# Fewer copied score pairs, and VectorE's side work placed between the score copies, in a fused attention and SwiGLU kernel

## Chip, cores and metric

One core of a Trainium2 chip runs the whole kernel. The metric is the time of one execution on the device in microseconds (us). PE is TensorE's matrix multiplier, PEld its weight load, DVE is VectorE, ACT is ScalarE, POOL is GpSimd, SP is the engine whose queue issues most DMAs.

## What is computed

```
xn = layernorm(x)                                  # x: 2048 tokens x 512
q, k, v = split(xn @ wqkv)                         # 32 heads of 16
o  = softmax(q @ k.T * 16**-0.5) @ v               # every head, 2048 x 2048 scores
s  = o @ wo
h  = silu(xn @ w_gate) * (xn @ w_up)               # 1792 wide
g  = silu(h @ w_down)
out = x + s * g
```

Inputs and outputs are float32. The kernel splits operands of a product into a rounded high part and the remaining low part and sums three products (high x high, high x low, low x high). Making such a pair costs DVE one copy (the rounding) and one subtraction.

## The kernel before

A first part (some 160 us) normalises x and projects q, k and v. Then comes the main loop, which is one instruction order written out by hand: each engine executes its instructions in the order in which the program emits them.

**Units and blocks.** Attention is cut into 32 units: 8 groups of 4 heads, times 4 slices of 512 queries. A unit goes over 16 tiles of 128 keys (kt). It is cut into 3 or 4 blocks of 4 to 6 key tiles, 100 blocks in all (`run`). A key tile has two pairs of heads, so a block of n tiles has 2n pairs, and each pair needs two score matmuls (128 x 512 each).

**Fill.** A block also carries f steps of other work, one step being two matmuls on the two row halves of the array (`both`, into `bankx` and `banky`): 24 steps for the gate and up projection of one 128-wide slice of the hidden layer, 21 for one token tile of the down projection, 9 or 12 for the output projection near the end. `events(n, f)` writes the order of a block as marks in slots: F is a fill step, D a direct pair, A and B the two halves of a copied pair. A slot is the time of one F or one D, half a slot that of an A or a B.

- A **direct** pair (D) goes into one of two double banks `score`, and ACT takes the exponential straight from there (L846).
- A **copied** pair (A, then B) goes one score at a time through the single bank `acc[1]` (`spare_bank`). DVE copies A out (L858); only then can B be written; DVE copies B out (L863). ACT takes the exponential of the copied pairs in place, at the end of the block (L865).

The tiles of exponentials, `pr`, come from a pool of 11 buffers; each is free again when `values` (L370) has multiplied it with v. `values` runs for the whole block after its events, tile by tile, with the copied pairs last. So PE's order is: events of a block, values of the block, events of the next.

The number of copied pairs follows from n and f; length = 2n + f:

| blocks | n | f | copied, of 2n |
|---|---|---|---|
| 31 | 5 | 24 | 1 |
| 23 | 5 | 21 | 2 |
| 22 | 6 | 24 | 3 |
| 7 | 6 | 21 | 4 |
| 11 | 4 | 12 | 3 |
| 2 | 4 | 9 | 4 |
| 2 and 2 | 4 | 21, 24 | 1, 0 |

That makes 214 copied pairs out of 1024.

**DVE's other work.** In a block with 24 fill steps the last step is followed by ACT's tanh (L212) and DVE's two gating steps (L213, L214), which free `bankx` and `banky`; then DVE splits the hidden slice `hh` (L169, L170, `split_hidden`) and the rows of w_down, `wd` (L147, L148, `split_wd`). `split_gu` (L136, L138) splits the gate and up weights of the next slice; its four pieces are emitted at every fourth fill step. At a unit's end `finish` turns `acc[0]`, divides by the softmax sum (`normalise`, L377, L380, L384), and for every second group turns the result back (L391) and, for the last group, splits it (`split_o`, L270, L271); all of that is emitted in one go after the second D of the next unit's first block. SP loads the weights two slices ahead (`load_gu`) and one slice of w_down (`load_wd`), whose single buffer `wdr` is free when `split_wd` has read it.

Of the kernel before, what the change touches and what calls it, by code (L numbers as in the profile page):

```python
# [9 lines left out]
F32 = mybir.dt.float32  # L10
# [9 lines left out]
P = 128  # L20
# [3 lines left out]
DH = 16  # L24
F = 1792
NB = 4
TB = S // NB
# [23 lines left out]
def tile_block(ctx: ExitStack, tc: tile.TileContext, x, wqkv, wo, w_gate, w_up, w_down, out):  # L51
# [71 lines left out]
    def load_gu(i):  # L123
# [3 lines left out]
            sp.dma_start(raw[j * HALF:(j + 1) * HALF], w[:, f * P:(f + 1) * P].rearrange("(c p) f -> p c f", p=HALF))  # L127
        gu[i] = [raw]

    def split_gu(i):  # L130
        raw = gu[i][0]
        hi = two.tile([P, DC, P], F32R, tag="guh", name="guh")
        lo = two.tile([P, DC, P], F32R, tag="gul", name="gul")
        gu[i] = (hi, lo)
        for h in (slice(0, DC // 2), slice(DC // 2, DC)):
            dve.tensor_copy(hi[:, h], raw[:, h])  # L136
            yield
            dve.tensor_sub(lo[:, h], raw[:, h], hi[:, h].bitcast(F32))  # L138
            yield

    def load_wd(i):
        raw = one.tile([P, D], F32, tag="wdr", name="wdr")
# [1 line left out]
        wdr[i] = raw  # L144

    def split_wd(f, i):
        dve.tensor_copy(wd[:, f, 0], wdr[i])  # L147
        dve.tensor_sub(wd[:, f, 1], wdr[i], wd[:, f, 0].bitcast(F32))  # L148

    def load_fx(b, j):  # L150
        for h in range(2):
# [13 lines left out]

    def split_hidden():
        while kept:
            f, i, ga = kept.pop(0)
            dve.tensor_copy(hh[:, f, 0], ga)  # L169
            dve.tensor_sub(hh[:, f, 1], ga, hh[:, f, 0].bitcast(F32))  # L170
            split_wd(f, i)

    halves = [slice(h * HALF, (h + 1) * HALF) for h in range(2)]

# [16 lines left out]
    def ffn(b):  # L191
        for grp, part in enumerate(GROUPS):
            nf = part.stop - part.start
            for f in range(nf):
                i = b * NF + part.start + f
                pieces = split_gu(i + 1) if i + 1 < NB * NF else iter(())
                if i + 2 < NB * NF:
                    load_gu(i + 2)
                hi, lo = gu.pop(i)
                n = 0  # L200
                for c in range(DC):
                    for wt, j in ((hi, 0), (hi, 1), (lo, 0)):
                        both(wt[:, c], fx[:, j, c], n == 0, n == 3 * DC - 1)
                        n += 1
                        if n % 4 == 2:
                            next(pieces, None)
                        if n == DC and i:
                            load_wd(i)
                        if n == 3 * DC:
                            th = one.tile([P, TB], F32, tag="th", name="th")  # L210
                            ga = two.tile([P, TB], F32, tag="ga", name="ga")
                            act(th, bankx, AF.Tanh, scale=0.5)  # L212
                            dve.scalar_tensor_tensor(ga, th, 1.0, bankx, op0=ALU.add, op1=ALU.mult)  # L213
                            dve.scalar_tensor_tensor(ga, ga, 0.5, banky, op0=ALU.mult, op1=ALU.mult)  # L214
                            kept.append((f, i, ga))
                            if now >= 0:
                                split_hidden()
                            if grp == 1 and f == nf - 1 and b + 1 < NB:
                                load_fx(b + 1, 0)
                                load_fx(b + 1, 1)  # L220
                            elif grp == 1 and f == nf - 1:
                                load_wo(0)
                        yield 3 * DC - n
            for t in range(NT):
                n = 0
                for f in range(nf):
                    for a, w in ((0, 0), (0, 1), (1, 0)):
                        both(hh[:, f, a, t * P:(t + 1) * P], wd[:, f, w], n == 0, n == 3 * nf - 1)
                        n += 1
                        if n == 3 * nf and grp == 0:  # L230
                            dve.tensor_copy(facc[:, t], bankx)
                            dve.tensor_add(facc[:, t], banky, facc[:, t])
                        elif n == 3 * nf:
                            y = two.tile([P, D], F32, tag="ga", name="y")
                            dve.tensor_add(y, bankx, facc[:, t])
                            dve.tensor_add(y, banky, y)
                            after.append(partial(store_gate, y, b * TB + t * P))
                            if b == NB - 1:
                                after.append(partial(next_out, t))
                        yield 3 * nf - n  # L240
# [132 lines left out]
    def normalise(u, first, last, between=None):  # L373
        g, b = divmod(u, NB)
        n = last - first
        o1 = late.tile([P, TB], F32, tag="o1", name="o1")
        dve.transpose(o1[:, :n], acc[0][:, first:last])  # L377
        ov = o1[:, :n].rearrange("p (c d) -> p c d", d=32)
        rl = late.tile([P, TB // 32], F32, tag="rl", name="rl")[:, :n // 32]
        dve.reciprocal(rl, ov[:, :, DH])  # L380
        if between:
            between()
        dst = on[b][:, first:last].rearrange("p (c s d) -> p c s d", s=2, d=DH)[:, :, g % 2]
        dve.tensor_mul(dst, ov[:, :, :DH], rl[:, :, None].to_broadcast([P, n // 32, DH]))  # L384

    def finish(u):
        g, b = divmod(u, NB)
        normalise(u, 0, TB)
        if g % 2:
            o2 = late.tile([P, TB], F32, tag="o2", name="o2")  # L390
            dve.transpose(o2, on[b])  # L391
            if g < NG - 1 or b == NB - 1:
                pool.dma_start(o_d[g // 2, b], o2)
            else:
                whole = (hh, wd, hh)[b].rearrange("p f j t -> p (f j) t")
                lhs[b, DT - 1] = whole[:, 2 * (DT - 1)], whole[:, 2 * DT - 1]
                split_o(lhs[b, DT - 1], o2)
                ready[b] += 1

    settled = mybir.DependencyInfo(mybir.DependencyClass.Sync, mybir.DependencyReason.DATA)  # L400
    units = NG * NB
# [45 lines left out]

    def events(n, f):
        length = 2 * n + f
        copied = max(0, 2 * n - max(2, (4 * length - 6) // 16 + 1)) if f else 0  # L450
        direct = 2 * n - copied
        gap = max(4, min(5, (length - 8) / max(1, direct - 2)))
        marks = [(0, "D"), (1, "D")] + [(7 + gap * i, "D") for i in range(direct - 2)]
        marks += [(4 + (length - 6) * i / (2 * copied), "AB"[i % 2]) for i in range(2 * copied)]
        marks.sort()
        out = []
        at = left = 0
        for t, kind in marks:
            while left < f - 1 and at < t:
                out.append("F")  # L460
                left += 1
                at += 1
            out.append(kind)
            at += 1 if kind == "D" else 0.5
        return direct, out + ["F"] * (f - left)


    with ExitStack() as pro:
        pc = pro.enter_context(tc.tile_pool(name="pc", bufs=1))
# [210 lines left out]
        for b in range(NB):  # L680
# [3 lines left out]
            for n, (make, i) in enumerate(slots):  # L684
# [9 lines left out]
                if b == 2 and n == 8:  # L694
                    load_wd(0)
                if not more and n == 2:
                    for _ in split_gu(0):
                        pass
                    for bank in acc:
                        dve.memset(bank, 0.0)  # L700
                if not more and n in (1, 3):
# [40 lines left out]
                if not more and n == 9:  # L742
# [6 lines left out]
                    for h in range(2):  # L749
                        dve.tensor_copy(selq[:, h * HALF:h * HALF + 1], s4)  # L750
                    fill(3 * DC)
                    low, high = [pps.tile([P, 512], F32, tag="ps", name="low") for _ in range(2)]
                    mm(high[:2 * NG * NB, :8], sel, row[:, :8], start=True, stop=True, skip_group_check=True)
                    mm(low[:HALF + 2, :8], selq, row[:, :8], start=True, stop=True, skip_group_check=True)
# [59 lines left out]

    now = 0
    split_hidden()
    ends = []

    def run(u, first, n):
# [4 lines left out]
        direct, todo = events(n, f)  # L824
        if now == 0:
            for _ in range(4):
                todo.insert(0, todo.pop(len(todo) - 1 - todo[::-1].index("F")))
        pairs = [(kt, j) for kt in range(first, first + n) for j in range(2)]
        straight, copies = pairs[:direct], pairs[direct:]
        probs, waiting = {}, []  # L830
# [4 lines left out]
            mm(bank, k[r, j, kc * P:(kc + 1) * P], q[r, j], start=True, stop=True)  # L835

        done = 0
        for e in todo:
            if e == "F":
                fill(1)  # L840
            elif e == "D":
# [10 lines left out]
            elif e == "A":  # L852
                kt, j = copies.pop(0)
                waiting.append((kt, j))
                scores(spare_bank, kt, j, 0)
                lower = True
                probs[kt, j] = ppool.tile([P, 2, TB], F32, tag="pr", name="pr")
                dve.tensor_copy(probs[kt, j][:, 0], spare_bank)  # L858
            else:
                kt, j = waiting[-1]  # L860
                scores(spare_bank, kt, j, 1)
                lower = False
                dve.tensor_copy(probs[kt, j][:, 1], spare_bank)  # L863
        for kt, j in waiting:
            act(probs[kt, j], probs[kt, j], AF.Exp, scale=0.25)  # L865
        out_splits()
        catch_up()
        values(u, range(first, first + n), probs)
# [51 lines left out]
    for t, c in ((2, 0), (2, 1), (2, 2), (3, 0)):  # L920
        products(t, c)
    for n in range(2):
        normalise(units - 1, n * half, (n + 1) * half, partial(low, 0) if n else None)
        turned.append(spare[:, n])
        dve.transpose(turned[n][:, :half], on[NB - 1][:, cols[n]])
        nc.scalar.copy(hi[:, cols[n]], turned[n][:, :half])
# [38 lines left out]
```

## Time and profile before

| | |
|---|---|
| median of 3 runs | 1583.88 us (1583.39 to 1585.63) |
| the profiled execution | 1583.19 us |
| its span, first to last instruction | 1581.4 us |
| busy: PE, PEld, DVE, ACT | 1520.2, 890.6, 829.0, 1098.2 us |
| direct exponentials | 810, 1027 ns each |
| exponentials of copied pairs | 214, 1060 ns each |
| score copies | 2 x 214, 690 and 692 ns each |

In the views, a row of the timeline gives start, duration, engine, line, operation, out<-in, shape and count of a run of like instructions, and in brackets the idle time of the engine before it with what ended that. Rows of PE overlap, since matmuls are pipelined. In a windows row the figures after the length are each engine's busy time, then the granted TensorE clock (1.00 is full), DMA share and GB/s.

### The profile page before, as it was taken

The numbers are of one execution on the slowest core, as the hardware profiler recorded it, in microseconds if no ns is written. First come the engines' busy times: TensorE is split into PE (matmuls) and PEld (weight loads), VectorE is DVE, ScalarE is ACT, GpSimd is POOL, SyncE is SP. The second block draws the span as 40 slices with busy tenths as digits, with TensorE's granted clock in tenths as the row PEclk, the third lists the DMA queues.
The fourth block names the chain that finished last, engine by engine and source line by source line (L and its number), as shares of the span: only waits on it lengthen the run. The fifth ranks groups of instructions, "written<-read, shape, count | busy, mean of one in ns | idle before, by whom it ended". The sixth has DMA issues, their size and how long they took to land.

```text
span 1581.4 us, 27925 instructions
## 1 busy us (share of the span) xinstructions
PE 1520.2 (96%) x11227; PEld 890.6 (56%) x11227; DVE 829.0 (52%) x1439; ACT 1098.2 (69%) x1235; POOL 89.4 (6%) x104
## 2 busy tenths in 40 slices
PE   9999799999999999999999999999999999888887
PEld 7787555555556555555565455565655555333333
DVE  5543454456546645554566355546554545554545
ACT  6633477777877777777877677787767776645543
POOL 4100100000000000000000000000000000001222
PEclk9999899999999999999999999999999999877978
DMA  6678521143624311444243034722321223122131
GB/s 220 235 251 245 129 67 32 38 114 76 138 64 117 80 32 31 102 100 112 68 108 75 11 72 100 154 74 71 92 65 37 66 58 91 51 84 80 61 100 48
DMA packets 126957, 148.18 MB, mean 94 GB/s; under 512 B 12524, under 2 KB 79340, under 8 KB 126052
## 3 DMA queue, kind: packets, MB, share of 16 engines
q1 hardware_dynamic: 121620, 125.79, 31.7%
q0 software_dynamic: 4912, 20.12, 3.4%
q8 instruction: 91, 1.49, 0.4%
q14 instruction: 46, 0.38, 0.1%
q10 hardware_dynamic: 288, 0.39, 0.1%
HBM read 106.68 MB, written 39.58 MB: 92 GB/s over the span
## 4 chain that ended last, share of the span: by engine, by line
PE 85%; DVE 8%; ACT 4%; issue 2%; DMA 1%; SPq 0%; DVEq 0%; ACTq 0%
PE acc L370 29%; PE bankx L182 18%; PE score L835 12%; PE banky L182 9%; PE acc L835 7%; PE ps L591 5%; ACT pr L846 3%; DVE pr L858 3%; PE ps L593 3%; DVE pr L863 1%; DVE o L377 1%; ACT pr L865 0%; DVE o L391 0%; PE acc L566 0%; DMA v_d<-vt 0%
## 5 line engine op out<-in xcount | busy, mean ns | idle before, releaser
L846 ACT ACTIVATE pr<-score 128x1024 f32<-128x1024 f32 x810 | 778.7, 1027 | 384.6 <-PE score L835 322.4
L370 PE MATMUL acc<-pr,vst 128*17 128x512 f32 x4096 | 510.0, 606 | 0.0
L835 PE MATMUL score<-qst,kst 50*128 50x512 f32 x1620 | 411.3, 419 | 0.0
L182 PE MATMUL banky<-fx,guh 64*128 64x512 f32 x896 | 319.8, 399 | 0.0
L182 PE MATMUL bankx<-fx,guh 64*128 64x512 f32 x896 | 312.3, 395 | 0.1
L370 PEld LDWEIGHTS acc<-pr,vst 128*17 128x17 f32 x4096 | 114.2, 98 | 343.5 <-issue 273.5
L858 DVE COPY pr<-acc 128x512 f32<-128x512 f32 x214 | 147.6, 690 | 206.0 <-PE acc L835 193.6
L835 PEld LDWEIGHTS score<-qst,kst 50*128 50x128 f32 x1620 | 187.3, 187 | 118.4 <-issue 74.0
L835 PE MATMUL acc<-qst,kst 50*128 50x512 f32 x428 | 200.0, 467 | 52.0 <-DVE pr L858 32.8
L863 DVE COPY pr<-acc 128x512 f32<-128x512 f32 x214 | 148.0, 692 | 139.2 <-PE acc L835 135.4
L865 ACT ACTIVATE pr<-pr 128x1024 f32<-128x1024 f32 x214 | 214.5, 1060 | 0.0
L182 PE MATMUL bankx<-wd,hh 64*128 64x512 f32 x672 | 205.8, 395 | 0.0
L182 PE MATMUL banky<-wd,hh 64*128 64x512 f32 x672 | 196.5, 394 | 0.0
L182 PEld LDWEIGHTS bankx<-fx,guh 64*128 64x128 f32 x896 | 167.6, 187 | 16.7 <-issue 0.9
L182 PE MATMUL bankx<-fx,gul 64*128 64x512 f32 x448 | 176.9, 395 | 0.0
L182 PE MATMUL banky<-fx,gul 64*128 64x512 f32 x448 | 176.6, 394 | 0.0
L182 PEld LDWEIGHTS banky<-fx,guh 64*128 64x128 f32 x896 | 165.7, 187 | 2.7
L835 PEld LDWEIGHTS acc<-qst,kst 50*128 50x128 f32 x428 | 81.4, 190 | 131.3 <-DVE pr L858 64.8
L213 DVE SCALAR_TENSOR_TENSOR ga<-th,bankx 128x512 f32<-128x512 f32 x56 | 38.5, 688 | 195.7 <-ACT th L212 195.7
L182 PEld LDWEIGHTS bankx<-wd,hh 64*128 64x128 f32 x672 | 124.1, 186 | 12.6
L182 PEld LDWEIGHTS banky<-wd,hh 64*128 64x128 f32 x672 | 124.3, 186 | 6.1
L182 PEld LDWEIGHTS bankx<-fx,gul 64*128 64x128 f32 x448 | 84.4, 188 | 6.9
(165 smaller groups left out, 1381.3 us busy)
## 6 DMA issues: line engine op xcount, KB each, us to landing
gur<-in_B_w_gate_dram SPq DMA_DIRECT2D x56, 256.0 KB
gur<-in_B_w_up_dram SPq DMA_DIRECT2D x56, 256.0 KB
wdr<-in_B_w_down_dram SPq DMA_DIRECT2D x56, 256.0 KB
kst<-k_d SPq DMA_DIRECT2D x192, 64.0 KB
qst<-q_d SPq DMA_DIRECT2D x192, 64.0 KB
fx<-xt_d SPq DMA_DIRECT2D x24, 512.0 KB
q_d<-parts SPq DMA_DIRECT2D x16, 512.0 KB
k_d<-parts SPq DMA_DIRECT2D x16, 512.0 KB
```

The source lines that it names most:

```text
L182: mm(banks[i], lhs[halves[i]], rhs[halves[i]], start=start, stop=stop)
L213: dve.scalar_tensor_tensor(ga, th, 1.0, bankx, op0=ALU.add, op1=ALU.mult)
L370: mm(acc[0][h * 32:h * 32 + DH + 1], v[:, kt % CT, h * (DH + 1):(h + 1) * (DH + 1)], probs[kt, h // 2][:, h % 2], start=kt == 0, stop=kt = ...
L377: dve.transpose(o1[:, :n], acc[0][:, first:last])
L591: mm(ps, w, a[:, c], start=n == 0, stop=n == 3 * DT - 1)
L593: mm(ps, a[:, c, tokens], w, start=n == 0, stop=n == 3 * DT - 1)
L835: mm(bank, k[r, j, kc * P:(kc + 1) * P], q[r, j], start=True, stop=True)
L846: act(probs[kt, j], score[done % 2], AF.Exp, scale=0.25)
L858: dve.tensor_copy(probs[kt, j][:, 0], spare_bank)
L863: dve.tensor_copy(probs[kt, j][:, 1], spare_bank)
L865: act(probs[kt, j], probs[kt, j], AF.Exp, scale=0.25)
```

## The change

Two things are changed. First, `events` copies fewer pairs: 2 instead of 3 in a (6, 24) block, 3 instead of 4 in (6, 21), 2 instead of 3 in (4, 12), 3 instead of 4 in (4, 9), none instead of 1 in (4, 21); 170 in all. (5, 24) and (5, 21) keep theirs. Second, DVE's splits of the weights and the steps of `finish` are no longer emitted where they arise. They go to a list, `chores`, with a cost in slots, and `run` takes them from the list where, by its count of slots, they end half a slot after the next score copy is due at the latest. What is left is emitted ahead of the block's last fill step, that is ahead of the tanh. The wd split now belongs to the block itself and is queued two steps before its end. `split_gu` rounds its tile with one copy of 1024 elements in place of two of 512. The split of `hh` follows the gating at once, as before.

```
     def events(n, f):
         length = 2 * n + f
-        copied = max(0, 2 * n - max(2, (4 * length - 6) // 16 + 1)) if f else 0
+        copied = max(0, 2 * n - max(2, (10 * length + 46) // 40)) if f else 0
...
     def split_gu(i):
...
-        for h in (slice(0, DC // 2), slice(DC // 2, DC)):
-            dve.tensor_copy(hi[:, h], raw[:, h])
-            yield
-            dve.tensor_sub(lo[:, h], raw[:, h], hi[:, h].bitcast(F32))
-            yield
+        chores.append((3, partial(dve.tensor_copy, hi, raw)))
+        for h in (slice(0, DC // 2), slice(DC // 2, DC)):
+            chores.append((3, partial(dve.tensor_sub, lo[:, h], raw[:, h], hi[:, h].bitcast(F32))))
+
+    def tidy(room=None):
+        while chores and (room is None or chores[0][0] <= room):
+            cost, work = chores.pop(0)
+            work()
...
     def split_wd(f, i):
-        dve.tensor_copy(wd[:, f, 0], wdr[i])
-        dve.tensor_sub(wd[:, f, 1], wdr[i], wd[:, f, 0].bitcast(F32))
+        chores.append((2, partial(dve.tensor_copy, wd[:, f, 0], wdr[i])))
+        chores.append((3, partial(dve.tensor_sub, wd[:, f, 1], wdr[i], wd[:, f, 0].bitcast(F32))))
...
     def ffn(b):
...
-                        if n % 4 == 2:
-                            next(pieces, None)
+                        if n == 3 * DC - 2 and now >= 0:
+                            split_wd(f, i)
...
     def finish(u):
         g, b = divmod(u, NB)
-        normalise(u, 0, TB)
+        chores.extend(normalise(u, 0, TB))
...
     def run(u, first, n):
...
+        copying = [t + 1.5 for t, e in todo if e in "AB"]
+        final = len(todo) - 1
+        free = 0
+        for at, (t, e) in enumerate(todo):
+            if at == final:
+                tidy()
...
                 dve.tensor_copy(probs[kt, j][:, 0], spare_bank)
+                free = copying.pop(0) + 3
...
+            while chores and at < final and (not copying or max(free, t) + chores[0][0] <= copying[0] + 0.5):
+                free = max(free, t) + chores[0][0]
+                chores.pop(0)[1]()
         for kt, j in waiting:
             act(probs[kt, j], probs[kt, j], AF.Exp, scale=0.25)
+        tidy()
```

More of the change, by code (lines that the diff above doesn't have):

```diff
@@ L128, in load_gu @@
         gu[i] = [raw]
+    chores = []
     def split_gu(i):
@@ L134, in split_gu @@
         gu[i] = (hi, lo)
+        chores.append((3, partial(dve.tensor_copy, hi, raw)))
         for h in (slice(0, DC // 2), slice(DC // 2, DC)):
-            dve.tensor_copy(hi[:, h], raw[:, h])
-            yield
-            dve.tensor_sub(lo[:, h], raw[:, h], hi[:, h].bitcast(F32))
-            yield
+            chores.append((3, partial(dve.tensor_sub, lo[:, h], raw[:, h], hi[:, h].bitcast(F32))))
[3 more added lines that the diff above has]
+            work()
+            if room is not None:
+                room -= cost
     def load_wd(i):
@@ L167, in split_hidden @@
         while kept:
[L168 to L171, printed above, removed]
+            f, ga = kept.pop(0)
+            chores.append((2, partial(dve.tensor_copy, hh[:, f, 0], ga)))
+            chores.append((3, partial(dve.tensor_sub, hh[:, f, 1], ga, hh[:, f, 0].bitcast(F32))))
     halves = [slice(h * HALF, (h + 1) * HALF) for h in range(2)]
@@ L195, in ffn @@
                 i = b * NF + part.start + f
-                pieces = split_gu(i + 1) if i + 1 < NB * NF else iter(())
+                if i + 1 < NB * NF:
+                    split_gu(i + 1)
                 if i + 2 < NB * NF:
@@ L214, in ffn @@
                             dve.scalar_tensor_tensor(ga, ga, 0.5, banky, op0=ALU.mult, op1=ALU.mult)
-                            kept.append((f, i, ga))
+                            kept.append((f, ga))
                             if now >= 0:
@@ L376, in normalise, with turn_out, rounded @@
         o1 = late.tile([P, TB], F32, tag="o1", name="o1")
-        dve.transpose(o1[:, :n], acc[0][:, first:last])
+        rl = late.tile([P, TB // 32], F32, tag="rl", name="rl")[:, :n // 32]
         ov = o1[:, :n].rearrange("p (c d) -> p c d", d=32)
-        rl = late.tile([P, TB // 32], F32, tag="rl", name="rl")[:, :n // 32]
-        dve.reciprocal(rl, ov[:, :, DH])
+        dst = on[b][:, first:last].rearrange("p (c s d) -> p c s d", s=2, d=DH)[:, :, g % 2]
+        yield 3, partial(dve.transpose, o1[:, :n], acc[0][:, first:last])
+        yield 1, partial(dve.reciprocal, rl, ov[:, :, DH])
         if between:
-            between()
-        dst = on[b][:, first:last].rearrange("p (c s d) -> p c s d", s=2, d=DH)[:, :, g % 2]
-        dve.tensor_mul(dst, ov[:, :, :DH], rl[:, :, None].to_broadcast([P, n // 32, DH]))
+            yield 3, between
+        yield 2, partial(dve.tensor_mul, dst, ov[:, :, :DH], rl[:, :, None].to_broadcast([P, n // 32, DH]))
     def finish(u):
         g, b = divmod(u, NB)
-        normalise(u, 0, TB)
+        chores.extend(normalise(u, 0, TB))
         if g % 2:
             o2 = late.tile([P, TB], F32, tag="o2", name="o2")
[L391 to L394, printed above, removed]
+            def turn_out():
+                dve.transpose(o2, on[b])
+                if g < NG - 1 or b == NB - 1:
+                    pool.dma_start(o_d[g // 2, b], o2)
+            chores.append((3, turn_out))
+            if g == NG - 1 and b < NB - 1:
                 whole = (hh, wd, hh)[b].rearrange("p f j t -> p (f j) t")
                 lhs[b, DT - 1] = whole[:, 2 * (DT - 1)], whole[:, 2 * DT - 1]
-                split_o(lhs[b, DT - 1], o2)
-                ready[b] += 1
+                def rounded():
+                    dve.tensor_copy(lhs[b, DT - 1][0], o2)
+                    ready[b] += 1
+                chores.append((2, rounded))
+                chores.append((3, lambda: dve.tensor_sub(lhs[b, DT - 1][1], o2, lhs[b, DT - 1][0].bitcast(F32))))
     settled = mybir.DependencyInfo(mybir.DependencyClass.Sync, mybir.DependencyReason.DATA)
@@ L459, in events @@
             while left < f - 1 and at < t:
-                out.append("F")
+                out.append((at, "F"))
                 left += 1
                 at += 1
-            out.append(kind)
+            out.append((at, kind))
             at += 1 if kind == "D" else 0.5
-        return direct, out + ["F"] * (f - left)
+        return direct, out + [(at + i, "F") for i in range(f - left)]
     with ExitStack() as pro:
@@ L696, in tile_block @@
                 if not more and n == 2:
-                    for _ in split_gu(0):
-                        pass
+                    split_gu(0)
+                    tidy()
                     for bank in acc:
@@ L816, in tile_block @@
     split_hidden()
+    split_wd(0, 0)
+    tidy()
     ends = []
@@ L826, in run @@
             for _ in range(4):
-                todo.insert(0, todo.pop(len(todo) - 1 - todo[::-1].index("F")))
+                todo.insert(0, todo.pop(max(i for i, (_, e) in enumerate(todo) if e == "F")))
         pairs = [(kt, j) for kt in range(first, first + n) for j in range(2)]
@@ L837, in run @@
         done = 0
-        for e in todo:
+        copying = [t + 1.5 for t, e in todo if e in "AB"]
[3 more added lines that the diff above has]
+            if at == final:
+                tidy()
             if e == "F":
@@ L863, in run @@
                 dve.tensor_copy(probs[kt, j][:, 1], spare_bank)
+                free = copying.pop(0) + 3
+            while chores and at < final and (not copying or max(free, t) + chores[0][0] <= copying[0] + 0.5):
+                free = max(free, t) + chores[0][0]
+                chores.pop(0)[1]()
         for kt, j in waiting:
             act(probs[kt, j], probs[kt, j], AF.Exp, scale=0.25)
+        tidy()
         out_splits()
@@ L922, in tile_block @@
     for n in range(2):
-        normalise(units - 1, n * half, (n + 1) * half, partial(low, 0) if n else None)
+        for _, work in normalise(units - 1, n * half, (n + 1) * half, partial(low, 0) if n else None):
+            work()
         turned.append(spare[:, n])
```

## The prediction

> **What bounds the kernel now.** I read the page's busy rows first, then the groups of instructions, then the timeline of one block of each kind, engine by engine.
>
> ```profile
> span 1581.4 us, 27925 instructions
> PE 1520.2 (96%) x11227; PEld 890.6 (56%) x11227; DVE 829.0 (52%) x1439; ACT 1098.2 (69%) x1235; POOL 89.4 (6%) x104
> L835 PE MATMUL acc<-qst,kst 50*128 50x512 f32 x428 | 200.0, 467 | 52.0 <-DVE pr L858 32.8 <-DVE pr L863 10.3 <-issue 6.1
> ```
>
> PE looks full, with 61.2 us of idle time, nearly all of it ahead of the score that goes into the single bank, and ended by DVE's copies. The timeline shows that more is lost than that. A (5, 24) block, which copies one pair, is dense:
>
> ```profile
> 505.75 0.74 PE L835 MATMUL score<-qst,kst 50*128 50x512 f32 x4
> 506.38 8.40 ACT L846 ACTIVATE pr<-score 128x1024 f32<-128x1024 f32 x9 [2.81 <-PE score L835]
> ...
> 513.96 4.49 PE L370 MATMUL acc<-pr,vst 128*17 128x512 f32 x40
> 518.38 0.74 PE L835 MATMUL score<-qst,kst 50*128 50x512 f32 x4
> 518.95 0.40 PE L182 MATMUL banky<-fx,guh 64*128 64x512 f32 x1
> ```
>
> From the first score to the values are 34 slots (10 pairs and 24 fill steps) in 8.21 us, so a slot is 0.24 us; the values take 4.42 us to the next block's first score, 0.88 us a key tile. That is my measure of a block without waiting. A (6, 21) block, which copies four pairs, against it:
>
> ```profile
> 721.64 0.73 PE L835 MATMUL score<-qst,kst 50*128 50x512 f32 x4
> ...
> 722.68 0.39 PE L835 MATMUL acc<-qst,kst 50*128 50x512 f32 x1
> ...
> 731.52 0.49 PE L835 MATMUL acc<-qst,kst 50*128 50x512 f32 x1
> ...
> 732.85 7.04 PE L370 MATMUL acc<-pr,vst 128*17 128x512 f32 x48
> 739.82 0.73 PE L835 MATMUL score<-qst,kst 50*128 50x512 f32 x4
> 724.38 0.69 DVE L863 COPY pr<-acc 128x512 f32<-128x512 f32 x1 [0.58 <-PE acc L835]
> ...
> 732.05 0.69 DVE L863 COPY pr<-acc 128x512 f32<-128x512 f32 x1 [0.59 <-PE acc L835]
> ```
>
> Its eight scores into the single bank run from 722.68 to 731.52. The copies follow each other every (732.05 - 724.38) / 6 = 1.28 us, of which 0.69 is the copy and 0.59 DVE waiting for the next score: score, copy, score, copy, with nothing overlapped. The marks ask for a score every (33 - 6) / 8 = 3.4 slots, 0.8 us. So this loop through one bank sets the block: 18.18 us, where 33 slots and six key tiles would take 33 x 0.24 + 6 x 0.88 = 13.2. PE's row still shows it nearly busy, because a matmul lasts 0.39 us or more while one starts every 0.12. So PE's own matmuls are the bound where copies lie far apart, and the round trip PE, DVE, PE wherever they come closer than 1.28 us (5.3 slots).
>
> **(6, 24): 22 blocks, three copies to two.** Before:
>
> ```profile
> 527.56 6.58 PE L370 MATMUL acc<-pr,vst 128*17 128x512 f32 x48
> 534.08 0.73 PE L835 MATMUL score<-qst,kst 50*128 50x512 f32 x4
> 528.71 1.03 ACT L846 ACTIVATE pr<-score 128x1024 f32<-128x1024 f32 x1 [1.44 <-PE acc L370]
> 530.10 2.95 ACT L865 ACTIVATE pr<-pr 128x1024 f32<-128x1024 f32 x3
> ```
>
> The block runs from 518.38 (above) to 534.08: 15.70 us. Events take 9.18 where 36 slots need 8.7; values 6.52 where six tiles need 5.3. The first loss is the bank: six scores spaced 30 / 6 = 5 slots, under the 5.3 of the loop. The second is ACT: the block's twelfth `pr` has only eleven buffers, so its exponential waits for the first tile of values (528.71, 1.15 after the values' start), and the tanh and three copied exponentials queue behind it until 533.05, 5.49 us after the start, when the last tile was due at 4.4. With two copies the marks lie 7.5 slots apart (1.8 us), which leaves half a microsecond beside each; the chores fill just that. The last exponential ends a third of 2.95 earlier, at 4.5: late by 0.1 to 0.2. New block: 36 x 0.24 + 5.3 + 0.2 = 14.2. Gain 1.5 each; times 21, without the loop's second block (below), 31.5.
>
> **(6, 21): 7 blocks, four to three.** Six scores into the bank: the first 1.04 us after the block's start, five rounds of 1.28 (the first a little shorter) to 7.4, then six slots where four took 1.33 (731.52 to 732.85): 1.8. Values start at 9.2 after 11.21. The values took 6.97; one exponential less in the queue, 0.95: 6.0. New 15.2, gain 3.0 each: 21. No chore falls into these blocks, so nothing else comes between the copies.
>
> **(4, 12): 11 blocks near the end, three to two.**
>
> ```profile
> 1434.94 0.73 PE L835 MATMUL score<-qst,kst 50*128 50x512 f32 x4
> ...
> 1442.49 0.79 PE L835 MATMUL acc<-qst,kst 50*128 50x512 f32 x1 [0.38 <-DVE pr L858]
> ...
> 1444.49 4.25 PE L370 MATMUL acc<-pr,vst 128*17 128x512 f32 x32
> 1448.66 0.73 PE L835 MATMUL score<-qst,kst 50*128 50x512 f32 x4
> 1441.00:1445.50 4.50, 3.98 (x20) 1.97 (x24) 2.61 (x5) 4.00 (x5) 0.00 (x0) 0.65 0.00 0
> ```
>
> 13.72 us for 20 slots (4.8) and four tiles (3.5). Six scores through the bank take until 7.55, and after some 6 us of that pace the granted clock falls (0.65 in the window's row), so three more slots take 2.0. With two copies there are four scores: 1.04 + 3 x 1.28 = 4.9; then five slots, where four took 1.33 above: 1.57, so values start at 6.4. The sixth direct score comes only after the last B, near 5.7; its exponential ends near 7.2 and the copied two near 9.2, when the last tile is due at 6.4 + 2.6. I take 0.3 for that: 6.4 + 3.5 + 0.3, rounded to 10.3, a gain of 3.4 each in nine: 30.6. Unless the clock still falls: 0.35 of PE's 3.98 us, 1.4 more each, 15 in all. I take none, since in the (6, 21) block above the slots fill 33 x 0.24 of 11.2 us (71%) and their pace held to the end, and here they would fill 4.8 of 6.4 (75%) after 4.8 of 9.6 (50%).
>
> [...]
>
> In two of the eleven a unit ends, and DVE does all of `finish` ahead of its first score copy:
>
> ```profile
> 1452.18 0.68 DVE L858 COPY pr<-acc 128x512 f32<-128x512 f32 x1
> ...
> 1465.63 0.73 PE L835 MATMUL score<-qst,kst 50*128 50x512 f32 x4
> ```
>
> From 1448.66 to 1465.63 are 16.97 us. The change leaves only the first transpose and the reciprocal ahead of the copy (the order of DVE's instructions shows that) and the rest after the last copy, beside the values: 10.3 again, gain 6.7 each: 13.4.
>
> **(4, 9): 2 blocks, four to three.**
>
> ```profile
> 1368.03 0.73 PE L835 MATMUL score<-qst,kst 50*128 50x512 f32 x4
> ...
> 1376.46 0.79 PE L835 MATMUL acc<-qst,kst 50*128 50x512 f32 x1 [0.36 <-DVE pr L858]
> ...
> 1381.18 5.17 PE L370 MATMUL acc<-pr,vst 128*17 128x512 f32 x32
> 1386.29 0.74 PE L835 MATMUL score<-qst,kst 50*128 50x512 f32 x4
> ```
>
> The score at 1376.46 is the sixth and would be the last of them: two rounds at the halved clock less, minus one slot more, 2.7, and half an exponential of 1.0 in the values: 3.2 of 18.26 us. The second one also loses `finish` ahead of its first copy, which above came 3.5 us into the block and could have come at 1.5: 2.0 more, 5.2. Together 8.4.
>
> **What is moved.** In the other blocks the copies stay. The six or so (5, 21) blocks after a unit's end lose a stall of some 0.6 us; I count 2. Chores ahead of the tanh delay the gating by at most the wd split, and that runs beside the last two fill steps and the tanh; DVE is otherwise idle there. In a dense block the gating has ended 2.1 us before the next fill step needs the banks:
>
> ```profile
> 516.09 0.69 DVE L214 SCALAR_TENSOR_TENSOR ga<-ga,banky 128x512 f32<-128x512 f32 x1
> 182.36 0.55 SPq L143 DMA_DIRECT2D wdr<-in_B_w_down_dram  x1
> 187.27 0.43 DVE L147 CAST wd<-wdr 128x512 fp32r<-128x512 f32 x1 [7.22 <-DMA wdr<-in_B_w_down_dram]
> 189.46 0.76 PE L835 MATMUL acc<-qst,kst 50*128 50x512 f32 x1 [6.08 <-issue]
> ```
>
> (516.78 against 518.95.) The wait that the change adds: the wd split now stands ahead of the gating, so a late `wdr` holds the gating, and through the banks PE's next fill step. SP issues `wdr` when the previous split has read it, and both move alike, so the lead stays, except where SP is behind, at a new group. There the load took 4.9 us (182.36 to 187.27). In the loop's second block PE stands waiting for it today, at the B score from 183 to 189.46. After, it would wait at that block's first fill step instead, with seven more slots still to do: 8 x 0.24, some 2 us worse, less 1 us of values. I count -1. At later group starts DVE does not wait today, and there is the cover of 2.1 us; I count nothing.
>
> Sum: 31.5 + 21 + 30.6 + 13.4 + 8.4 + 2 - 1 = 106 us. The profiled execution took 1583.19 (span 1581.4, 0.7 below the median): 1477.
>
> **Rivals.** *The busy row is right.* If PE were as full as its row says, at most its 61.2 us of idle time could go: 1522. Against it speaks the (6, 21) block, which alone takes 5 us more than its slots and tiles, seven times over. [...] Chance 0.05. *ACT takes over.* More direct pairs wait for the two double banks. In the dense block nine exponentials in a row take 8.40 us, 0.93 each, where marks 4 slots apart ask for one every 0.96; in the new (6, 24) block the marks are 3.8 apart (0.91), so ACT is just behind. If each cost its whole 1.03 us in turn, a (6, 24) block would be 0.6 + 12 x 1.03 + 0.6 for the tanh + 0.9 for the last tile + half of the 1.44 us that ACT idles for the twelfth buffer: 15.2; a (4, 12) block 0.6 + 8 x 1.03 + 3.5 = 12.3. Gains 22 x 0.5 + 21 + 9 x 1.4 + 2 x 4.7 + 8.4 = 62: 1521. Chance 0.08. *Slower.* The wd wait decides: in every one of 55 slices DVE would stand at the wd split until `wdr` lands, then PE at the banks. That needs a landing more than 2.1 us after the gating's old place; to undo 106 us it must cost PE 1.9 us per slice, and 2 us gives 1477 + 110 = 1587. Against it: today DVE waits for `wdr` once. Chance 0.06. *Without effect:* the order of instructions shows the copies gone, so only by chance; 1583, 0.02.
>
> **Numbers.** 0.79 for the forecast, 1477. Downward: no lateness of the last tiles (22 x 0.2 + 11 x 0.3 = 8), rounds of 1.18 instead of 1.28 (7 x 0.5 + 11 x 0.3 = 7), and unit ends in (6, 24) blocks, which I priced like the others (up to 2 us in each of four): 23 in all, 1454. The clock that still falls (15) and a (6, 24) block that keeps half its loss (16) give 1508; the two rivals of smaller gain reach 1521 and 1522. Range 1455 to 1525. Faster by over 0.2% 0.92, within it 0.02, slower 0.06; 0.2% is about what runs of this kernel can tell apart (they lie 0.14% apart).
>
> **What would show it.** The twelve-pair (6, 24) blocks at 14.2 us, (6, 21) at 15.2, (4, 12) at 10.3 with the clock at 1.00; PE's idle time ahead of the single bank's score well under 52 us; the first fill step of the second block waiting for the gating. Wrong, if direct scores wait for ACT instead, if DVE's wait for `wdr` recurs, or if the clock near the end stays low.

## The result: 1484.4 us, 6.3% faster

Median of four runs 1484.43 us (1483.68 to 1487.12), against 1584.1 (1583.39 to 1585.63) for the kernel before; the ratio is 0.937, 95% interval 0.936 to 0.939. Forecast was 1477 in a range of 1455 to 1525. The profiled execution took 1483.91 us, 99.3 less than that of before.

The page of the changed kernel, the same rows as before, with the granted clock over the span and the fill that uses `bankx` first:

```profile
span 1482.1 us, 27795 instructions
PE 1448.6 (98%) x11227; PEld 873.7 (59%) x11227; DVE 765.3 (52%) x1295; ACT 1091.7 (74%) x1235; POOL 89.8 (6%) x104
...
PEclk9999999999999999999999999999999999999999
...
L188 PE MATMUL bankx<-fx,guh 64*128 64x512 f32 x896 | 313.4, 396 | 6.5 <-DVE ga L220 6.4
...
L853 PE MATMUL acc<-qst,kst 50*128 50x512 f32 x340 | 144.8, 426 | 17.9 <-DVE pr L881 12.8
```

PE's idle time ahead of the single bank's score fell from 52.0 to 17.9 us. But PE's idle time in all fell only from 61.2 to 33.5; the other 71.6 of the 99 us were inside rows that already counted as busy, with the same 11227 matmuls. The clock stays at 0.9 or more in every slice. And a wait has moved: the 6.4 us of PE at `bankx`, for the gating step, are one single wait, in the loop's second block, in place of the 6.1 us that PE stood there before.

For a sum by blocks, a block is counted from the last value matmul of the block before it to its own last value matmul, and the blocks of a kind are added up. The loop's first block has none before it and is left out.

| kind | blocks | before | after | gained | forecast |
|---|---|---|---|---|---|
| (6, 24) | 21 | 331.4 | 306.6 | 24.8 | 31.5 |
| (6, 24), second of the loop | 1 | 23.6 | 23.6 | 0.0 | -1 |
| (6, 21) | 7 | 130.8 | 108.6 | 22.2 | 21 |
| (4, 12) | 11 | 157.8 | 118.4 | 39.4 | 44 |
| (4, 9) | 2 | 38.6 | 30.0 | 8.6 | 8.4 |
| (5, 21) | 23 | 278.8 | 274.8 | 4.0 | 2 |
| (5, 24), (4, 21), (4, 24) | 34 | 422.6 | 422.1 | 0.5 | 0 |

The gains add up to 99.5 us, which is all of it. Of these, 68 us lie in the events and 31 in the values. In the (6, 24) blocks of the first row it is 5.3 and 19.5: there most of the gain is at the block's end, where ACT has one copied exponential fewer to do before the last tiles of values.

The timeline of PE in the (6, 21) block that was shown before, now with six scores into the bank:

```profile
707.23 0.50 PE L853 MATMUL acc<-qst,kst 50*128 50x512 f32 x1
...
708.51 0.50 PE L853 MATMUL acc<-qst,kst 50*128 50x512 f32 x1
...
709.79 0.50 PE L853 MATMUL acc<-qst,kst 50*128 50x512 f32 x1
...
711.63 6.09 PE L377 MATMUL acc<-pr,vst 128*17 128x512 f32 x48
717.65 0.73 PE L853 MATMUL score<-qst,kst 50*128 50x512 f32 x4
```

The round is the same 1.28 us; there are two fewer of it, and one exponential less holds the values up (6.02 us where it was 6.97).

A (6, 24) block on PE, with the weight load of its last direct score, then on ACT:

```profile
781.53 0.73 PE L853 MATMUL score<-qst,kst 50*128 50x512 f32 x4
...
789.76 0.50 PE L853 MATMUL score<-qst,kst 50*128 50x512 f32 x2
...
790.43 5.64 PE L377 MATMUL acc<-pr,vst 128*17 128x512 f32 x48
796.00 0.73 PE L853 MATMUL score<-qst,kst 50*128 50x512 f32 x4
789.76 0.19 PEld L853 LDWEIGHTS score<-qst,kst 50*128 50x128 f32 x2 [0.38 <-ACT pr L869]
```

```profile
788.69 1.94 ACT L869 ACTIVATE pr<-score 128x1024 f32<-128x1024 f32 x2
791.58 1.02 ACT L869 ACTIVATE pr<-score 128x1024 f32<-128x1024 f32 x1 [0.95 <-PE acc L377]
792.50 0.59 ACT L219 ACTIVATE th<-bankx 128x512 f32<-128x512 f32 x1
792.98 2.01 ACT L893 ACTIVATE pr<-pr 128x1024 f32<-128x1024 f32 x2
```

14.47 us: events 8.90, values 5.57. The last direct score starts at 789.76; its weight load had to wait for the first of the two exponentials that began at 788.69. The twelfth exponential still starts 1.15 us after the values.

A (4, 12) block on PE, and the windows of the block just before it:

```profile
1444.19 0.73 PE L853 MATMUL score<-qst,kst 50*128 50x512 f32 x4
...
1449.10 0.50 PE L853 MATMUL acc<-qst,kst 50*128 50x512 f32 x1 [0.17 <-DVE pr L881]
...
1450.69 4.15 PE L377 MATMUL acc<-pr,vst 128*17 128x512 f32 x32
1454.78 0.73 PE L853 MATMUL score<-qst,kst 50*128 50x512 f32 x4
```

```profile
1433.60:1440.00 6.40, 5.93 (x42) 3.89 (x40) 2.77 (x4) 4.57 (x5) 1.98 (x3) 1.00 0.42 117
1440.00:1444.20 4.20, 4.20 (x35) 0.95 (x34) 1.39 (x2) 3.17 (x4) 2.46 (x2) 1.00 1.03 361
```

10.59 us, with the last of four bank scores 4.9 us in. The block before it takes 10.59 us too, with the clock at 1.00 throughout.

The new wait, in the list of waits (total, times, longest) and on DVE and PE at a group's start:

```profile
DVE wd L891 <- DMA wdr<-in_B_w_down_dram: 41.2, 7, 13.4
```

```profile
346.73 0.43 DVE L891 CAST wd<-wdr 128x512 fp32r<-128x512 f32 x1 [5.80 <-DMA wdr<-in_B_w_down_dram]
347.19 0.69 DVE L891 TENSOR_TENSOR wd<-wdr,wd 128x512 fp32r<-128x512 f32 x1
347.80 0.68 DVE L220 SCALAR_TENSOR_TENSOR ga<-th,bankx 128x512 f32<-128x512 f32 x1
348.58 0.69 DVE L221 SCALAR_TENSOR_TENSOR ga<-ga,banky 128x512 f32<-128x512 f32 x1
```

```profile
348.59 0.43 PE L188 MATMUL bankx<-fx,guh 64*128 64x512 f32 x1
349.32 0.49 PE L188 MATMUL banky<-fx,guh 64*128 64x512 f32 x1 [0.30 <-DVE ga L221]
```

DVE waits for `wdr` in 7 places, where it did in one, 41.2 us in all. Most of that is covered; here the gating ends at 349.27 and PE's second fill matmul starts with it.

### The profile page after: what moved, and what is told of

It reads as the page before. It is cut to its first block, busy times and chain, and to the rows that moved or that the text cites. A ratio compares the mean times of both kernels' runs of the same rounds, so it can differ in the third digit from the quotient of the medians.

```text
span 1482.1 us, 27795 instructions
## 1 busy us (share of the span) xinstructions
PE 1448.6 (98%) x11227; PEld 873.7 (59%) x11227; DVE 765.3 (52%) x1295; ACT 1091.7 (74%) x1235; POOL 89.8 (6%) x104
## 4 chain that ended last, share of the span: by engine, by line
PE 93%; DVE 3%; ACT 1%; DMA 1%; SPq 1%; issue 0%; DVEq 0%; ACTq 0%
PE acc L377 30%; PE bankx L188 23%; PE score L853 15%; PE banky L188 10%; PE ps L606 6%; PE acc L853 5%; PE ps L608 3%; DVE pr L881 1%; DMA wdr<-in_B_w_down_dram 1%; SPq L100 1%; DVE pr L887 1%; ACT pr L869 0%; PE acc L581 0%; ACT pr L893 0%; DMA v_d<-vt 0%
## 5 line engine op out<-in xcount | busy, mean ns | idle before, releaser
L869 ACT ACTIVATE pr<-score 128x1024 f32<-128x1024 f32 x854 | 813.6, 1028 | 293.2 <-PE score L853 258.9
L377 PE MATMUL acc<-pr,vst 128*17 128x512 f32 x4096 | 478.8, 596 | 0.0
L853 PE MATMUL score<-qst,kst 50*128 50x512 f32 x1708 | 420.5, 419 | 0.1
L188 PE MATMUL banky<-fx,guh 64*128 64x512 f32 x896 | 312.8, 396 | 0.4 <-DVE ga L221 0.3
L881 DVE COPY pr<-acc 128x512 f32<-128x512 f32 x170 | 117.5, 691 | 189.4 <-PE acc L853 188.7
L887 DVE COPY pr<-acc 128x512 f32<-128x512 f32 x170 | 117.6, 692 | 109.7 <-PE acc L853 99.6
L893 ACT ACTIVATE pr<-pr 128x1024 f32<-128x1024 f32 x170 | 172.8, 1064 | 0.0
L853 PE MATMUL acc<-qst,kst 50*128 50x512 f32 x340 | 144.8, 426 | 17.9 <-DVE pr L881 12.8
L188 PEld LDWEIGHTS bankx<-wd,hh 64*128 64x128 f32 x672 | 124.8, 187 | 13.8
L853 PEld LDWEIGHTS acc<-qst,kst 50*128 50x128 f32 x340 | 63.7, 187 | 54.7 <-DVE pr L881 26.9
```

The costliest lines, as they stand in the source:

```text
L188: mm(banks[i], lhs[halves[i]], rhs[halves[i]], start=start, stop=stop)
L377: mm(acc[0][h * 32:h * 32 + DH + 1], v[:, kt % CT, h * (DH + 1):(h + 1) * (DH + 1)], probs[kt, h // 2][:, h % 2], start=kt == 0, stop=kt = ...
L869: act(probs[kt, j], score[done % 2], AF.Exp, scale=0.25)
```

## Experiments

The theory: the round trip through the single bank bounds every block whose copies are asked for faster than every 1.28 us, so the number of copies carries the gain; the placing of DVE's work counts where unit ends stand ahead of a first copy. Rivals: DVE's other work made the copies late, so that the placing carries it; ScalarE takes over.

**The counts alone**, on the kernel before:

```
-        copied = max(0, 2 * n - max(2, (4 * length - 6) // 16 + 1)) if f else 0
+        copied = max(0, 2 * n - max(2, (10 * length + 46) // 40)) if f else 0
```

> The kernel before with the new number of copied pairs alone; VectorE's splits and unit ends stay where they were. If the round trip through the single bank is what bounded the long blocks, this carries most of the gain: (6, 24) near 14.5 us, (6, 21) near 15.2, (4, 12) near 10.6, and only the unit ends ahead of a first copy stay: about 2 us in each of three late blocks, 0.6 in six (5, 21) blocks, and up to 2 in the (6, 24) blocks that open a unit. 1495, from 1488 to 1503. If VectorE was late because of its other work, so that the placing carries the gain: over 1530.

1493.67 us, ratio 0.942 (0.940 to 0.944). The median blocks: (6, 24) at 14.46 us, (6, 21) at 15.38, (4, 12) at 10.59, the same as with the whole change. What is missing is at unit ends: the two (4, 12) blocks that open a unit take 13.53 and 14.52 instead of 10.6, the (4, 9) block 17.3 instead of 14.7, and (5, 21) stays at its old sum of 278.8. The (6, 24) kind comes to 304.2, even 2.4 less than with the whole change. So the number of copies is worth some 91 of the 100 us by itself.

**The placing alone**, the changed kernel with the old formula (the same line, reversed).

> The changed kernel with the old number of copied pairs; only the placing of VectorE's splits and unit ends is new. By the round trip: (6, 21) stays near 18.2 us and (4, 12) near 13.7, (6, 24) loses at most 0.5 of its 15.7; what goes is the unit ends in the late blocks, some 15 to 20 us in all: 1565, from 1555 to 1575. If the placing carries the gain: under 1530.

1577.58 us, ratio 0.9954 (0.9938 to 0.9971): faster by 7 us (0.5%), less than the 15 to 20 expected, and outside the range of 1555 to 1575. (6, 21) and (4, 12) keep their 18.5 and 13.8 us, which falls in with the round trip and against the rival. The unit ends go as expected ((4, 12) blocks 13.8 instead of 17.0 and 17.8), but two other (4, 12) blocks take 1.7 and 2.2 us more. The (6, 24) blocks get worse as well, 334.5 for 331.4, with 17.34, 16.98, 16.67 and 16.49 us where a group starts; and the loop's second block takes 25.4 for 23.6. The wait for `wdr` is the part that I had left out of this expectation.

**The w_down split back behind the gating:**

```
-                        if n == 3 * DC - 2 and now >= 0:
-                            split_wd(f, i)
...
             chores.append((3, partial(dve.tensor_sub, hh[:, f, 1], ga, hh[:, f, 0].bitcast(F32))))
+            split_wd(f, i)
...
```

> The changed kernel with the w_down split put back behind the gating and the split of the hidden slice. If the gating is held by the load of w_down where a new group starts, the blocks after those starts (events of 10.4, 10.1 and 10.15 us at 347, 662 and 821 us) fall to the 9.4 of their kind and the loop's second block loses about 1 us: 3 us in all, 1481, from 1479 to 1484. If that wait comes from something else, they stay and the time is the same.

1480.64 us (1479.9 to 1482.66), ratio 0.9346 (0.933 to 0.936). The (6, 24) blocks after group starts fall from 15.46, 15.13 and 15.20 to 14.44, 14.58 and 14.47, and the second block from 23.65 to 23.03. The list of waits now has

```profile
DVE wd L889 <- DMA wdr<-in_B_w_down_dram: 6.9, 1, 6.9
```

one such wait, as before the change. So the placing ahead of the tanh costs 3 us in these four blocks (the medians lie 3.8 apart), and the wait is the cause: it goes, and the blocks shorten with it.

**One copied pair fewer** in all four kinds:

```
+        copied -= 1 if (n, f) in ((6, 24), (6, 21), (4, 12), (4, 9)) else 0
```

> The changed kernel with one more copied pair turned direct in each (6, 24), (6, 21), (4, 12) and (4, 9) block. Each class is read by itself in the trace. If the round trip still bounds (6, 21), (4, 12) and (4, 9) and ScalarE bounds (6, 24): (6, 24) 0.3 to 0.5 us longer than 14.5, (6, 21) 13.8 instead of 15.2, (4, 12) 9.5 instead of 10.6, (4, 9) some 3 less: 1465, from 1458 to 1474. If ScalarE has already taken over everywhere: all classes longer, over 1490.

1471.2 us, ratio 0.9286 (0.927 to 0.930), inside the expected range but 6 over its middle. (6, 21) 14.17 us (13.8 expected), (4, 12) 9.66 (9.5), (4, 9) 4 less, and (6, 24) 15.08, 0.6 longer (0.3 to 0.5 expected). In the (6, 24) block ACT is now behind, on PE's timeline:

```profile
793.25 0.50 PE L854 MATMUL score<-qst,kst 50*128 50x512 f32 x2 [0.15 <-ACT pr L870]
...
794.16 0.50 PE L854 MATMUL score<-qst,kst 50*128 50x512 f32 x2 [0.42 <-ACT pr L870]
...
794.83 5.34 PE L377 MATMUL acc<-pr,vst 128*17 128x512 f32 x48
```

So the change stands at ScalarE's edge in (6, 24) blocks and short of it in the other three.

**Twelve buffers** for the exponentials:

```
-PROBS = 11
+PROBS = 12
...
```

> The changed kernel with 12 instead of 11 buffers for the exponentials (the room comes from letting the second transposed tile of a unit's end share the first one's buffer, and from keeping the reciprocals in that tile). If the twelfth exponential of a six-tile block waits for a buffer and holds ScalarE's queue, and with it the last tile of values: the values of (6, 24) blocks fall from 5.05 to 4.8 us and of (6, 21) blocks from 5.50 to 4.8, events unchanged: 11 us, 1473, from 1470 to 1477. If the values wait for ScalarE's pace alone: no difference over 2 us.

1470.19 us, ratio 0.9277 (0.925 to 0.931). Counted, as in the expectation, to the start of the last value matmul, the values take 4.75 us in both kinds (5.05 and 5.50 before); to the next block's first score, as above, they take 5.27 (5.57 and 6.03). The events are as they were. ACT in such a block runs on through the values' start at 783.79, where it had waited 0.95 us:

```profile
782.05 2.85 ACT L871 ACTIVATE pr<-score 128x1024 f32<-128x1024 f32 x3
784.76 0.63 ACT L219 ACTIVATE th<-bankx 128x512 f32<-128x512 f32 x1
785.24 2.03 ACT L895 ACTIVATE pr<-pr 128x1024 f32<-128x1024 f32 x2
```

It gained 14 us, 3 more than expected; block by block 7 of them lie in (6, 24), 6 in (6, 21), 1 in (4, 12).

**The best counts**, with the split behind the gating:

```
+        copied -= 1 if (n, f) in ((6, 21), (4, 12), (4, 9)) else 0
```

> The w_down split behind the gating, and one copied pair fewer in (6, 21), (4, 12) and (4, 9) alone; (6, 24) stays at two. If the classes are independent, what each gained in the run with one fewer everywhere adds to the run with the split behind the gating: 1480.6 - 8.9 - 9.6 - 8 = 1454, from 1450 to 1459. If they share ScalarE's time across blocks, less: over 1462.

1453.28 us, ratio 0.9165 (0.914 to 0.919): the parts add.

**Two fewer** in these three kinds:

> The same with two copied pairs fewer in (6, 21), (4, 12) and (4, 9): 1, 0 and 1 are left. Now the last direct score waits for ScalarE at 0.93 us an exponential. By that: (6, 21) 0.5 us longer than with one fewer, (4, 12) 0.4 longer, (4, 9) about 1 shorter, so 6 more than the run with one fewer in these classes: 1460, from 1456 to 1466. If the round trip through the single bank is still the bound: shorter again, under 1450.

1472.0 us, ratio 0.9285 (0.926 to 0.931), well over the 1460 expected. ScalarE is the bound, as expected, but dearer: (4, 12) 10.48 us for 9.65, (6, 21) 15.0 for 14.17. Two (6, 21) blocks took 16.7. In one of them, on PE:

```profile
706.52 0.50 PE L852 MATMUL score<-qst,kst 50*128 50x512 f32 x2 [0.41 <-ACT pr L868]
707.43 0.50 PE L852 MATMUL score<-qst,kst 50*128 50x512 f32 x2 [0.42 <-ACT pr L868]
```

With its fill used up, PE does one direct pair per exponential here, and right behind it the granted clock falls to 0.50 for 3.4 us of the values (the windows stand in the last section). One (4, 12) block took 12.2 us and one (4, 9) block 11.3.

**Every score copy twice**, on the kernel before:

```
                 dve.tensor_copy(probs[kt, j][:, 0], spare_bank)
+                dve.tensor_copy(probs[kt, j][:, 0], spare_bank)
...
                 dve.tensor_copy(probs[kt, j][:, 1], spare_bank)
+                dve.tensor_copy(probs[kt, j][:, 1], spare_bank)
```

> The kernel before with every score copy on VectorE made twice over, which does the same work again and changes no result. If the loop score, copy, score is the bound of the blocks with close copies, each round grows from 1.28 to 1.89 us: (6, 24) 3.1 us longer, (6, 21) 4.3, (4, 12) 3 to 3.5, (4, 9) 4.3, (5, 21) about 1, (5, 24) not at all: 168 us in all, 1752, from 1725 to 1780. If VectorE, busy for half the time, has the copies beside other work: under 1610.

1821.39 us (one run), above the expected range of 1725 to 1780. (5, 24) blocks, whose copies lie 14 slots apart, keep their 12.62 us; (5, 21) takes 1.6 more (1 expected), (6, 24) 3.6 (3.1), (6, 21) 8 (4.3), (4, 12) 5.7 (3 to 3.5). For each copy that was doubled that is 0, 0.4, 0.6 and 1.0 us in the first four, with the copies 14, 6.3, 5 and 3.4 slots apart: the cost grows as they come closer. DVE's timeline in a (6, 21) block shows the round at 2.01 us, a little over the 1.89, and later at 2.30:

```profile
796.59 0.69 DVE L858 COPY pr<-acc 128x512 f32<-128x512 f32 x1 [2.06 <-PE acc L835]
797.32 0.69 DVE L859 COPY pr<-acc 128x512 f32<-128x512 f32 x1
798.60 0.69 DVE L864 COPY pr<-acc 128x512 f32<-128x512 f32 x1 [0.59 <-PE acc L835]
799.32 0.69 DVE L865 COPY pr<-acc 128x512 f32<-128x512 f32 x1
800.61 0.69 DVE L858 COPY pr<-acc 128x512 f32<-128x512 f32 x1 [0.59 <-PE acc L835]
...
802.91 0.69 DVE L864 COPY pr<-acc 128x512 f32<-128x512 f32 x1 [0.88 <-PE acc L835]
...
805.21 0.69 DVE L858 COPY pr<-acc 128x512 f32<-128x512 f32 x1 [0.88 <-PE acc L835]
```

The second step goes with the granted clock, the third figure from the end in the windows of the same block:

```profile
797.00:802.00 5.00, 2.83 (x16) 1.21 (x13) 3.72 (x6) 2.63 (x3) 0.00 (x0) 0.89 0.56 135
802.00:807.00 5.00, 4.46 (x16) 2.64 (x18) 2.79 (x5) 1.90 (x2) 0.00 (x0) 0.50 0.00 0
```

**All together**: the best counts, 12 buffers, and one copied pair in (4, 9).

> The run with the best counts, with 12 buffers besides, and one copied pair in (4, 9) blocks instead of two. If the buffer wait and the counts act in different blocks, the (6, 24) blocks gain the 0.3 us each that they gained from 12 buffers, 22 x 0.3 = 6.6, the (6, 21) blocks nothing more (their values are at 4.75 already), the (4, 9) blocks 1 each: 1445, from 1441 to 1449. If the twelfth buffer only moves ScalarE's wait to the score banks: 1453 again.

1444.48 us (1443.02 to 1444.83), ratio 0.912 (0.911 to 0.914): 40 us faster than the change.

## Why the prediction was right, and where it was off

**The bound.** Right: doubled copies lengthen blocks by how close the copies stand, and the counts alone bring 91 us. Not all of that is the round trip. Most of the 31 us in the values are the second loss that the prediction named, exponentials that queue on ACT at a block's end, and the run with twelve buffers took more of them.

**(6, 21) and (4, 9).** The (6, 21) block that was worked out came to 15.19 us, as forecast; the seven lie between 15.2 and 16.1. (4, 9) came to 8.6 against 8.4 with some luck: 3.0 and 5.7 in the two blocks, where 3.2 and 5.2 were forecast.

**(6, 24).** The step that was too large: 14.2 forecast, 14.47 measured. Of the 0.27, 0.2 are events (8.90 for 8.7), because the tenth direct score waits for ACT; I had named that ("just behind") under the rival and put nothing of it into the sum. 24.8 instead of 31.5 for the kind also holds the next point.

**The wait for `wdr`.** The mechanism was named, and its place in the loop's second block was right (PE waits at the first fill step; 0.0 gained, -1 forecast). Wrong was to count nothing at later group starts for the 2.1 us of cover: three blocks lost 0.5 to 1.0 us each, which came back with the split behind the gating. A `wdr` issued at a group's start lands some 5 us later (341.75 to 346.73 in the changed kernel), and the split is now wanted before that.

```profile
341.75 0.54 SPq L150 DMA_DIRECT2D wdr<-in_B_w_down_dram  x1
```

**(4, 12).** 10.59 instead of 10.3: the last tile's wait was 0.5 us, not 0.3. The forecast also took the gain of one block for nine, but two of the eleven had kept the clock at 1.00 before and took 12.87 and 12.23 us, so they had less to lose; the others lost the halved clock (0.50 for 3.4 to 10.2 us of each) along with the round trip. The clock held at 1.00 in ten of the eleven, as taken, though the share of slots over a block, by which it was taken, is no safe sign (last section). In the eleventh (12.45 us) DVE's first copy is still behind splits of the output projection, which the change does not move, and the clock fell to 0.50 for 3.4 us (1405.15 to 1408.57).

**Unit ends.** The two (4, 12) blocks came to 10.6, as the others. By the counts alone they stand at 13.5 and 14.5, so 3 to 4 us of each gain were the placing's, the rest the counts'.

**The rivals.** The busy row was no ceiling: 99 us went where 61 were idle. ACT took over nowhere, beyond the 0.2 us in (6, 24), but it is the next bound, as the runs with fewer copies show. The slower case asked for waits in 55 slices; there were 7, mostly covered.

## What to carry to other kernels

Where one engine fills a single buffer that another must empty, measure the round trip in the timeline and compare it with the distance at which the schedule asks for it: here PE's busy row read 96% with such a loop in it, and each round of it took its whole 1.28 us. Read a change of schedule class by class of block; then gains and losses add, and the next step (fewer copies in three kinds, one buffer more) follows from the same table. A step that is moved ahead on an engine's queue takes its DMA wait with it (the w_down split: 7 waits, 41.2 us, ahead of the tanh, and one of 6.9 behind the gating): ask which work behind it can then be late.

## What the runs showed of the hardware

The granted clock fell to 0.50 in the block with doubled copies (802.00 to 813.70 in its windows), whose longest idle stretch of PE is this one:

```profile
800.07 0.50 PE L835 MATMUL acc<-qst,kst 50*128 50x512 f32 x1 [1.04 <-DVE pr L865]
```

The share of slots in a block's events does not tell when the clock falls. Of the (4, 12) blocks of before, nine, filled to between 38 and 52%, met a clock of 0.50, and two at 52 and 56% stayed at 1.00; its (6, 21) blocks, at 63 to 71%, stayed at 1.00; with the copies doubled the one shown was at some 43% (7.9 us of slots in 18.6) and fell to 0.50. But the (6, 21) block of 16.7 us that was shown in part, at 82%, did too. Its windows, at its end:

```profile
701.60:705.00 3.40, 3.40 (x32) 2.93 (x30) 0.69 (x1) 3.40 (x5) 0.00 (x0) 1.00 1.05 207
705.00:708.40 3.40, 2.43 (x16) 0.83 (x17) 0.20 (x1) 3.30 (x4) 0.00 (x0) 1.00 0.25 91
708.40:711.80 3.40, 3.40 (x20) 0.76 (x16) 1.18 (x2) 1.99 (x3) 0.00 (x0) 0.50 0.02 5
```

In the 3.40 us ahead of the fall PE has 16 matmuls where it has 32 in the 3.40 us before, and the two gaps shown above are 0.41 and 0.42 us. What makes the clock fall is not shown.
